# Gated attention and Mish layer on one core: Mish on 1024 columns, early heads kept in DRAM, VectorE exponentials in whole and half sets

## The chip, the core and the metric

The kernel runs on one core of a Trainium2 chip. The core has TensorE (PE, matrix products into PSUM banks of 512 32-bit columns), ScalarE (ACT, activation functions), VectorE (DVE, elementwise work), GpSimd (POOL) and SyncE (SP), which issues most DMAs. Each engine runs its own instructions strictly in the order in which the program lists them and waits on semaphores for the others. The metric is device time in microseconds (us) of one execution, the median of several runs; lower is better.

## The reference

```python
def _A_ref(x, wqkv, wo):            # H = 32 heads of Dh = 20, S = 2048, D = 640
    qkv = (x @ wqkv).reshape(B, S, 3, H, Dh).transpose(2, 0, 3, 1, 4)
    q, k, v = qkv[0], qkv[1], qkv[2]
    p = softmax(einsum("bhqd,bhkd->bhqk", q, k) * Dh ** -0.5, axis=-1)
    o = einsum("bhqk,bhkd->bhqd", p, v)
    return o.transpose(0, 2, 1, 3).reshape(B, S, D) @ wo

def _B_ref(x, w1, b1, w2):          # F = 1536
    h = einsum("bsd,df->bsf", x, w1) + b1
    sp = log1p(exp(-abs(h))) + where(h > 0, h, 0)
    return einsum("bsf,fd->bsd", h * tanh(sp), w2)

g = sigmoid((x * gate_w).sum(-1, keepdims=True))
return g * _A_ref(x, wqkv, wo) + (1 - g) * _B_ref(x, w1, b1, w2)
```

All inputs and the output are bf16. The activation `h * tanh(softplus(h))` is Mish. With n = e^h (e^h + 2) it is h * n / (n + 2), which is how the kernel computes it: one exponential and one reciprocal.

## The kernel before

**Attention.** The 32 heads are taken four at a time (p = 0 to 7) and the 2048 queries in four blocks qc of 512. A pair (p, qc) is a *group*; there are 32 groups G, first p = 0 to 5 with all four qc each, then for each qc the pairs p = 6 and p = 7. A group has 16 key blocks j of 128 keys and four heads t, 64 *units* in all. One unit is a score matmul (`Sp`, 128 keys by 512 queries, one PSUM bank), the exponential of it, and a matmul of V against the result, which adds into `acc` (L1160; V carries a column of ones, so the softmax sums come along). The maximum isn't subtracted; a bound on the scores is worked out on the way, and `attention_with_maximum` is a fallback that isn't entered with these inputs.

**The stream of iterations.** Units are packed into iterations that alternate between three and two banks of scores (`WIDTHS`, tiles `S0` and `S1`). Iteration i+1's scores are issued (`emit_qk`), then ScalarE takes iteration i's exponential in one instruction of 1536 or 1024 columns (`emit_exp`, L1108), then the V matmuls whose exponentials are issued (`emit_pv`), then VectorE work that is due, then fill-in matmuls on TensorE (`pump`).

**Heads on VectorE.** In groups 1 to 30 one key block of the 16 is left to VectorE: in some three-bank iterations ScalarE takes only two banks, and VectorE reads the third (`jv_read`, L735) into a 16-bit integer tile. When two heads are there, `jv_steps` makes the exponential from integer and 16-bit arithmetic, seven instructions on 128x1024 (L753 to L775). The score bank is free for the iteration after the next when both engines have read it.

**Other work between the iterations.** Projections of q, k, v, the Mish layer (`h_chain`, `mish_steps`, `b_chain`) and the output projection (`wo_chain`) are chains of matmul pieces with a start and a due iteration; `pump` places them in TensorE's order. VectorE's longer work is cut into steps with deadlines (`steps`, `run_slow`), which a planner with fixed costs (the list `T`) places into VectorE's order. Where TensorE would go quiet, matmuls of constants (`busy`, L1033) are put in. All of it is decided when the program is built, so every engine's order is fixed.

**Mish** works on one block of 128 rows of F by 512 tokens at a time: 12 blocks for each of four token blocks c. TensorE makes `h` (5 matmuls, L607), VectorE adds the bias (L618), ScalarE makes e^h (L548), and VectorE does nine instructions (L556 to L588): n and n + 2 in 32 bits, products of two and of four denominators so that only 128 columns need a reciprocal (L570), and the way back. The results lie in *cells* (48 tiles of 128x512 bf16). `b_chain` multiplies them with W2 and frees them.

**Outputs of heads.** At a group's end `normalise` turns `acc` over (L1128), divides by the sums and turns it back into a cell (L1146), which stays there until `wo_chain` uses it, late in the kernel, because the output projection of a query block needs all eight p.

Of the kernel before, what the change touches and what calls it, by code (L numbers as in the profile page):

```python
# [9 lines left out]
P = 128  # L10
# [31 lines left out]
def attention_with_maximum(tc, A_wqkv, b_dram, out2d, xT, VA, wo_sb, g_t, ident, pool):  # L42
# [10 lines left out]
    with tc.For_i(0, H, 1, name="heads") as h:  # L53
# [20 lines left out]
        with tc.For_i(0, S, P, name="queries") as q0:  # L74
# [9 lines left out]
            mx = pool["m"].tile([P, 4], F32, tag="r", name="mx")  # L84
# [23 lines left out]
            on = pool["m"].tile([P, DH], BF16, tag="h", name="on")  # L108
# [42 lines left out]
def kernel(  # L151
# [18 lines left out]
    FT = F // P  # L170
    NS = S // P
# [9 lines left out]
    JV_SETS = {G: 1 for G in range(1, 31)}  # L181
    JV_BIAS = 32
    JV_GAPS = {1: (4, 2, 4, 2), 2: (3, 2, 2, 2, 2, 2, 2, 2)}
    N_CAP = 1.0e9
    NCELL = 48
# [21 lines left out]
    mp = ctx.enter_context(tc.tile_pool(name="mp", bufs=2))  # L207
# [21 lines left out]
    E_dve = [consts.tile([P, 4, QC], BF16, tag=f"E_dve{i}", name=f"E_dve{i}") for i in range(2)]  # L229
    w_dve = consts.tile([P, 2, QC], F16, tag="w_dve")  # L230
    VB = consts.tile([P, 2, H, DH + 1], BF16, tag="VB")
    u_dve = consts.tile([P, 2, QC], F16, tag="u_dve")
    b_dram = tc.dram_tile([S, D], BF16, name="b_dram")
    acc = accpool.tile([P, QC], F32, tag="acc")
# [17 lines left out]
    def load_w1(k, eng=nc.sync):  # L252
        if k < 4 * NQC:
            i = k % 4
            w1t[k] = w1p.tile([P, KT, 3 * P], BF16, tag="w1t", name="w1t")
            eng.dma_start(out=w1t[k][:, :, :], in_=w1rows[:, :, 3 * P * i : 3 * P * (i + 1)])
# [43 lines left out]
    for G, (p, qc) in enumerate(groups):  # L300
        first.setdefault(p, G)

    mine_of = [[NS - 1 - k for k in range(JV_SETS.get(G, 0))] for G in range(len(groups))]
    units = [
        (G, p, qc, j, t)
        for G, (p, qc) in enumerate(groups)
        for j in range(NS)
        if j not in mine_of[G]
        for t in range(4)
    ]  # L310
    unit_at = {(G, j): k for k, (G, _, _, j, t) in enumerate(units) if t == 0}


# [3 lines left out]
    taken_by, iters_start = {}, {}  # L317
    while pos < len(units):
        i = len(iters)
        G = units[pos][0]  # L320
        n = min(WIDTHS[i % len(WIDTHS)], len(units) - pos)
        x = None
        got = taken_by.setdefault(G, [])
        sets_here = len(mine_of[G])
        if n == 3 and len(got) < 4 * sets_here:
            since = i - (got[-1][0] if got else iters_start.get(G, i))
            if since >= JV_GAPS[sets_here][len(got)] and units[pos + 1][0] == G:
                mine = {units[pos][4], units[pos + 1][4]}
                k, slot = divmod(len(got), 4)
                left = [t for t in range(4) if t not in [y for _, y in got[4 * k :]]]  # L330
                t = min(left, key=lambda t: (t in mine, t))
                got.append((i, t))
                x = (G, units[pos][1], k, t, slot)
                n = 2
        for k in range(pos, pos + n):
            iters_start.setdefault(units[k][0], i)
        iters.append((pos, n))
        extra.append(x)
        pos += n
    assert all(len(taken_by[G]) == 4 * len(mine_of[G]) for G in range(len(groups)))  # L340
# [17 lines left out]
    in_mish = [0]  # L358
    b_done = [0] * NQC
# [14 lines left out]
    NS_SCORES, NS_SET, NS_SCORES_SEEN, NS_EXP_SEEN, NS_MISH_EXP = 330.0, 320.0, 430.0, 180.0, 519.0  # L374
    NS_SEEN = 250.0
    QUEUE = 700.0
# [42 lines left out]
    def steps(start, parts, deadline, line=None):  # L419


        seq[0] += 1
        slow.append([deadline, seq[0], start, deque(parts), line])

# [120 lines left out]
    def mish_steps(ft, c, h):  # L545
        e = mp.tile([P, QC], F32, tag="e", name="e")
        r = mp.tile([P, QC], F32, tag="r", name="r")
        nc.scalar.activation(e[:, :], h[:, :], ACT.Exp)  # L548
        T["act"] += 519.0
        V = nc.vector  # L550
        d = r.rearrange("p (a b) -> p a b", a=2)
        Q = slice(0, P)

        def n_and_d():

            V.scalar_tensor_tensor(out=e, in0=e, scalar=2.0, in1=e, op0=ALU.add, op1=ALU.mult)  # L556
            V.tensor_scalar(out=r, in0=e, scalar1=N_CAP, scalar2=2.0, op0=ALU.min, op1=ALU.add)

        def products():

            V.scalar_tensor_tensor(
                out=e.rearrange("p (a b) -> p a b", a=2),
                in0=e.rearrange("p (a b) -> p a b", a=2),
                scalar=N_CAP, in1=d[:, ::-1, :], op0=ALU.min, op1=ALU.mult,
            )
            V.tensor_tensor(out=r[:, 2 * P :], in0=r[:, 0 : 2 * P], in1=r[:, 2 * P :], op=ALU.mult)
            V.tensor_tensor(out=r[:, Q], in0=r[:, 2 * P : 3 * P], in1=r[:, 3 * P :], op=ALU.mult)

        def invert():
            V.reciprocal(out=r[:, Q], in_=r[:, Q])  # L570

        def of_two():
            V.tensor_tensor(
                out=r[:, P : 3 * P].rearrange("p (a b) -> p a b", a=2),
                in0=r[:, 2 * P :].rearrange("p (a b) -> p a b", a=2)[:, ::-1, :],
                in1=r[:, Q].unsqueeze(1).to_broadcast([P, 2, P]),
                op=ALU.mult,
            )
            V.tensor_tensor(  # L579
                out=e.rearrange("p (a b) -> p a b", a=2),  # L580
                in0=e.rearrange("p (a b) -> p a b", a=2),
                in1=r[:, P : 3 * P].unsqueeze(1).to_broadcast([P, 2, 2 * P]),
                op=ALU.mult,
            )

        def last():
            t = taken.pop((ft, c))
            V.tensor_tensor(out=t, in0=h, in1=e, op=ALU.mult)  # L588
            act[(ft, c)] = t
            in_mish[0] -= 1  # L590
# [3 lines left out]
            [(1150, n_and_d), (1400, products), (920, invert), (1110, of_two), (690, last)],  # L594
            T["act"] + 9000.0,
        )

    def h_chain(ft, c, start, due):
        box = {}
        bank = opener(box, QC)  # L600

        def piece(kt):
            if kt == 0:
                in_mish[0] += 1
                taken[(ft, c)] = cells.pop()
# [3 lines left out]
                lhsT=w1t[4 * c + ft // 3][:, kt, (ft % 3) * P : (ft % 3 + 1) * P],  # L609
# [5 lines left out]
        def finish():  # L615
            h = mp.tile([P, QC], F32, tag="h", name="h")
            evac(740)
            nc.vector.tensor_scalar(  # L618
                out=h, in0=box["ps"][:, :], scalar1=b1f[:, ft : ft + 1], scalar2=None, op0=ALU.add
            )  # L620
            ready_h.append((T["dve"] + 200.0, lambda: mish_steps(ft, c, h)))
            if ft % 3 == 2:
                load_w1(4 * c + ft // 3 + 2)

        def ready():
            return in_mish[0] < 2 and len(cells) > CELLS_KEPT
# [43 lines left out]
    ots = {}  # L670
    wo_sb = [None]

    def wo_chain(s, half, start, due, ps_list, base=None, dst=None):
# [17 lines left out]
        def finish():  # L691
# [12 lines left out]
            if dst is None and half == 1:  # L704
                nc.sync.dma_start(out=out2d[s * P : (s + 1) * P, :], in_=ots[s][:, :])

        def ready():
            return all((p, c) in normalised for p in ps_list)
# [10 lines left out]
    jv_set = {}  # L719
# [3 lines left out]
    halves = {}  # L723
    jv_emitted = set()

    def jv_read(G, k, t, slot, ps, full):

        if slot == 0:
            n = jv_set[(G, k)] = len(jv_set)
            assert n < 2 or n - 2 in jv_emitted, (G, k)  # L730
        n = jv_set[(G, k)]
# [4 lines left out]
            out=E_dve[n % 2].bitcast(I16)[:, slot, :], in0=ps, scalar1=ROUND,  # L736
            scalar2=ROUND - 512.0 * JV_BIAS, op0=ALU.add, op1=ALU.subtract,
        )
        if slot % 2 == 1:
            left = (it_at(G + 1) - now[0]) * 1115.0  # L740
            due = T["act"] + (min(left - 4000.0, 9000.0) if k < len(mine_of[G]) - 1 else left - 4000.0)
            steps(T["dve"], jv_steps(G, k, slot // 2), due, "exp")

    def jv_steps(G, k, half):
        V = nc.vector
        E, w, u = (
            t.rearrange("p a n -> p (a n)")
            for t in (E_dve[jv_set[(G, k)] % 2][:, 2 * half : 2 * half + 2, :], w_dve, u_dve)
        )
# [24 lines left out]
        def scale():  # L774
            V.tensor_tensor(out=e, in0=e, in1=wi, op=ALU.add)  # L775
            halves[(G, k)] = halves.get((G, k), 0) + 1
            if halves[(G, k)] == 2:
                jv_at[(G, k)] = T["dve"] + NS_SEEN

        return [  # L780
            (380, mantissa), (380, exponent), (640, square), (380, factor), (380, factor2),
            (640, product), (640, scale),
# [155 lines left out]
    m0, m1 = it_at(1) + 10, it_at(G7[NQC - 1] - 1)  # L938
# [139 lines left out]
    def emit_qk(i):  # L1078
# [10 lines left out]
        if extra[i] is not None:  # L1089
            G, p, k, t, slot = extra[i]  # L1090
            todo.append((G, p, mine_of[G][k], t))
# [31 lines left out]
    def normalise(G, p, qc):  # L1123
# [20 lines left out]
        def turn():  # L1144
            normalised.add((p, qc))
            nc.vector.transpose(out=OT[(p, qc)][:, :], in_=t2[:, :])  # L1146

# [5 lines left out]
    jv_in = [0]  # L1153

    def emit_set(G, p, qc, j, moving, full, VB=None):
        n = pv_sets[0]
        T["pe"] = max(T["pe"], full, T["acc"] if n == 0 else 0.0) + NS_SET
        worked(T["pe"] - NS_SET, 215.0, 1.1)
        for t in range(4):
            nc.tensor.matmul(  # L1160
                acc[32 * t : 32 * t + DH + 1, :],
                lhsT=VA[:, j, 4 * p + t, :] if VB is None else VB[:, 4 * p + t, :],
                rhs=moving(t),
# [5 lines left out]
        if n == NS - 1:  # L1169
            normalise(G, p, qc)  # L1170
            pv_sets[0] = 0
            jv_in[0] = 0

    def emit_jv(G, p, qc):
        k = jv_in[0]
        n = jv_set[(G, k)]
        jv_in[0] += 1
        jv_emitted.add(n)
        E = E_dve[n % 2]
# [202 lines left out]
```

## Time and profile before

| | us |
|---|---|
| median of 3 runs | 934.8 (934.23 to 937.8) |
| the profiled execution | 934.48 |
| its span, first to last instruction | 932.7 |
| ScalarE busy | 908.5 |
| VectorE busy | 741.8 |
| TensorE busy (ends are modelled) | 866.7 |
| of that, matmuls of constants (L1033) | 110.3 |

A row of a group in the profile reads: line, engine, operation, output <- input by tile name, shapes and types, count; then the union of the busy time of the group in us and the mean ns of one instruction; then the idle time of the engine just before them with what ended it. A row of a window reads: stretch, its length, and for PE, PEld (weight load), DVE, ACT and POOL the busy us with the count of instructions, then the granted TensorE clock, the DMA share and GB/s. ScalarE's first exponential starts at 10.56 us and its last ends at 921.84 us; what follows is the last group's normalisation, projection and store. The granted TensorE clock is 0.996 of full speed.

### The profile page before, as it was taken

Reading aid. Unit: us, or ns where it says so; the run is one execution under the profiler, and the core shown is the slowest. Engines: PE = TensorE matmul, PEld = TensorE weight load, DVE = VectorE, ACT = ScalarE, POOL = GpSimd, SP = SyncE. Lnnn points to the kernel's source line nnn. Section 1 sums busy time; section 2 is a strip of 40 time slices with the busy share of each in tenths; the row PEclk is TensorE's granted clock in tenths of the full one; section 3 lists DMA queues with packets and bytes.
Section 4 is the critical chain, followed back from the end, with each engine's and each line's share of the span. In section 5 each row is a group of like instructions: output and inputs, shape, how many; then the busy total and the mean of one; then the engine's idle time right before and its main releaser. Section 6 shows DMA issues by size and latency. Waiting matters only on the chain.

```text
span 932.7 us, 15290 instructions
## 1 busy us (share of the span) xinstructions
PE 866.7 (93%) x6184; PEld 303.9 (33%) x6184; DVE 741.8 (80%) x1398; ACT 908.5 (97%) x873; POOL 24.4 (3%) x39
## 2 busy tenths in 40 slices
PE   8999999999999999999999999999999999999996
PEld 4433333223333333323332233233323233333332
DVE  4468888988888988889988889888888886786633
ACT  6999999999999999999999999999999999999995
POOL 5000100000000000000000000000000000000000
PEclk9999999999999999999999999999999999999998
DMA  9000100000100010001110001010000000100100
GB/s 270 32 1 1 31 1 22 17 6 1 31 1 22 2 31 1 22 1 50 29 23 16 22 1 31 3 48 2 21 1 22 1 9 8 43 8 9 43 29 31
DMA packets 25635, 22.00 MB, mean 24 GB/s; under 512 B 10088, under 2 KB 24312, under 8 KB 25560
## 3 DMA queue, kind: packets, MB, share of 16 engines
q1 hardware_dynamic: 22808, 14.28, 5.6%
q0 software_dynamic: 1520, 5.94, 2.1%
q8 instruction: 49, 0.80, 0.3%
q10 hardware_dynamic: 1232, 0.76, 0.3%
q14 instruction: 26, 0.21, 0.1%
HBM read 15.73 MB, written 5.24 MB: 22 GB/s over the span
## 4 chain that ended last, share of the span: by engine, by line
ACT 65%; issue 16%; PE 14%; DVE 3%; DMA 1%; POOL 1%; ACTq 0%; POOLq 0%
ACT E L1108 62%; PE Sp L1093 5%; ACT e L548 3%; PE acc L1160 3%; PE ps L638 2%; PE ps L490 2%; DMA wv<-in_A_wqkv_dram 1%; PE ps L683 1%; PE ps L607 1%; PE ps L1033 1%; PE ps L518 1%; DVE ot L1332 0%; DVE h L618 0%; POOL xs L273 0%; DVE T L1128 0%
## 5 line engine op out<-in xcount | busy, mean ns | idle before, releaser
L1108 ACT ACTIVATE E<-Sp 128x1024 bf16<-128x1024 f32 (+1 forms) x819 | 890.3, 1268 | 6.6 <-PE Sp L1093 3.7
L1093 PE MATMUL Sp<-qT,kT 32*128 32x512 bf16 x2048 | 326.1, 382 | 51.3 <-ACT E L1108 35.7
L1093 PEld LDWEIGHTS <-kT 32*128 32x128 bf16 x2048 | 108.6, 91 | 292.5 <-issue 253.8
L1160 PE MATMUL acc<-E,VA 128*21 128x512 bf16 x1928 | 191.2, 386 | 1.3 <-DVE T L1128 1.1
L735 DVE TENSOR_SCALAR E_dve<-Sp 128x512 int16<-128x512 f32 x120 | 82.8, 690 | 40.4 <-PE Sp L1093 39.5
L1033 PE MATMUL ps<-busy 128*128 128x512 bf16 x357 | 110.3, 384 | 0.0
L1160 PEld LDWEIGHTS <-VA 128*21 128x21 bf16 x1928 | 47.6, 88 | 108.8 <-issue 108.5
L607 PE MATMUL ps<-xT,w1t 128*128 128x512 bf16 x240 | 75.5, 385 | 0.0
L638 PE MATMUL ps<-w_sb,cell 128*128 128x320 bf16 x384 | 74.9, 302 | 0.0
L490 PE MATMUL ps<-xT,wkp 128*128 128x512 bf16 x155 | 48.4, 384 | 1.7 <-DVE xT L456 0.8
L490 PE MATMUL ps<-xT,wqp 128*128 128x512 bf16 x155 | 49.5, 384 | 0.0
L683 PE MATMUL ps<-wo_sb,cell 128*128 128x320 bf16 x248 | 48.2, 302 | 0.0
L618 DVE TENSOR_SCALAR h<-ps,b1f 128x512 f32<-128x512 f32 x48 | 35.8, 746 | 14.6 <-PE ps L607 14.1
L570 DVE RECIPROCAL r<-r 128x128 f32<-128x128 f32 x48 | 45.4, 946 | 0.6
L1128 DVE STREAM_TRANSPOSE T<-acc 128x512 f32<-128x512 f32 x32 | 22.9, 716 | 26.7 <-PE acc L1160 26.5
L772 DVE TENSOR_TENSOR w_dve<-w_dve,u_dve 128x1024 bf16<-128x1024 f16 x60 | 41.1, 685 | 0.9
L775 DVE TENSOR_TENSOR E_dve<-E_dve,w_dve 128x1024 int16<-128x1024 int16 x60 | 41.1, 685 | 0.9
L1033 PEld LDWEIGHTS <-busy 128*128 128x128 bf16 x357 | 26.9, 97 | 44.6 <-issue 35.1
L763 DVE TENSOR_TENSOR w_dve<-w_dve 128x1024 f16<-128x1024 f16 x60 | 41.0, 683 | 0.0
L638 PEld LDWEIGHTS <-cell 128*128 128x128 bf16 x384 | 29.3, 97 | 34.5 <-issue 28.0
L548 ACT ACTIVATE e<-h 128x512 f32<-128x512 f32 x48 | 34.9, 727 | 0.1
L579 DVE TENSOR_TENSOR e<-e,r 128x512 f32<-128x512 f32 x48 | 33.2, 692 | 1.6
(105 smaller groups left out, 651.1 us busy)
## 6 DMA issues: line engine op xcount, KB each, us to landing
w1t<-in_B_w_dram SPq DMA_DIRECT2D x14, 480.0 KB, 4.0
b_dram<-Bt SPq DMA_DIRECT2D x4, 640.0 KB, 3.2
out_dram<-ot SPq DMA_DIRECT2D x14, 160.0 KB, 1.8
xs<-in_A_x_dram POOLq DMA_DIRECT2D x3, 640.0 KB, 7.0
w_sb<-in_B_w_dram POOLq DMA_DIRECT2D x1, 1920.0 KB, 12.9
ws<-in_A_wqkv_dram SPq DMA_DIRECT2D x13, 100.0 KB, 4.0
w1t<-in_B_w_dram POOLq DMA_DIRECT2D x2, 480.0 KB, 8.8
wo_sb<-in_A_wo_dram SPq DMA_DIRECT2D x4, 200.0 KB
```

The costliest lines, as they stand in the source:

```text
L490: nc.tensor.matmul(box["ps"][:, :], lhsT=wpad[:, kt, :, :].rearrange("p h d -> p (h d)"), rhs=xT[:, kt, chunk * QC : (chunk + 1) * QC], st ...
L548: nc.scalar.activation(e[:, :], h[:, :], ACT.Exp)
L570: V.reciprocal(out=r[:, Q], in_=r[:, Q])
L607: nc.tensor.matmul(box["ps"][:, :], lhsT=w1t[4 * c + ft // 3][:, kt, (ft % 3) * P : (ft % 3 + 1) * P], rhs=xT[:, kt, c * QC : (c + 1) * QC ...
L638: nc.tensor.matmul(box["ps"][:, :], lhsT=act[(ft, c)][:, u * P : (u + 1) * P], rhs=w2_sb[:, ft, half * HALF : (half + 1) * HALF], start=(f ...
L683: nc.tensor.matmul(box["ps"][:, :], lhsT=OT[(p, c)][:, u * P : (u + 1) * P], rhs=wo_sb[0][:, p, cols], start=(k == 0), stop=(k == len(ps_l ...
L735: S_reader[0] = nc.vector.tensor_scalar(out=E_dve[n % 2].bitcast(I16)[:, slot, :], in0=ps, scalar1=ROUND, scalar2=ROUND - 512.0 * JV_BIAS, ...
L772: V.tensor_tensor(out=w.bitcast(BF16), in0=w, in1=u, op=ALU.mult)
L1033: nc.tensor.matmul(ps[:, 0:n], lhsT=busy[:, :], rhs=busy_row(n), start=True, stop=True)
L1093: nc.tensor.matmul(ps[:, k * QC : (k + 1) * QC], lhsT=kT[p][32 * t : 32 * t + 32, j * P : (j + 1) * P], rhs=qT[G][32 * t : 32 * t + 32, :] ...
L1108: exp = nc.scalar.activation(E[:, 0 : n * QC], S_of.pop(i)[:, 0 : n * QC], ACT.Exp, scale=LN2 / 512.0)
L1160: nc.tensor.matmul(acc[32 * t : 32 * t + DH + 1, :], lhsT=VA[:, j, 4 * p + t, :] if VB is None else VB[:, 4 * p + t, :], rhs=moving(t), st ...
```

## The change

- *Heads on VectorE.* Groups 1 to 31 have one whole set of four heads (key block 15). The groups 1, 2, 4, 5 and every second one to 29, sixteen in all, have a half set too: two heads of key block 14, whose other two heads stay on ScalarE. A set is computed when all its heads are read, on 128x2048 (whole) or 128x1024 (half), in the same seven steps. The units' head order now turns with the key block, and the head that VectorE takes is always another than the two beside it. A whole set's V matmuls go in when it is ready, a half set's at the group's end.
- *Mish* works on two blocks of 128 rows at once, 1024 columns: `h` is bf16, one exponential for both, n + 2 in fp16, the way back in 16 bits where marked. The reciprocal still takes 128 columns at a time. The buffers other than `h` exist once instead of twice, so the next pair's exponential is issued only after `share` of the one before (`mish_free`). W1 is loaded in tiles of 256 columns instead of 384.
- *Outputs of heads* p = 0 to 5 are stored to DRAM (`heads_dram`, 128 KB each, 24 in all) by SP right after they are normalised, and loaded back eight iterations before the group of p = 7 of their query block. There are 40 cells instead of 48.
- *The planner* has new costs, a longer look-ahead for VectorE's steps (`QUEUE`) and later deadlines.

```diff
-    JV_SETS = {G: 1 for G in range(1, 31)}
+    JV_DOUBLE = (1, 2, *range(4, 5), *range(5, 30, 2))
+    JV_PARTS = {G: 2 if G in JV_DOUBLE else 1 for G in range(1, 32)}
+    JV_HEADS = (4, 2)
-    JV_GAPS = {1: (4, 2, 4, 2), 2: (3, 2, 2, 2, 2, 2, 2, 2)}
-    N_CAP = 1.0e9
-    NCELL = 48
+    JV_GAPS = {1: (6, 2, 2, 2), 2: (5, 2, 2, 2, 2, 2)}
+    N_CAP = 16382.0
+    NCELL = 40
...
-    mp = ctx.enter_context(tc.tile_pool(name="mp", bufs=2))
+    mp = ctx.enter_context(tc.tile_pool(name="mp", bufs=1))
+    hp = ctx.enter_context(tc.tile_pool(name="hp", bufs=2))
...
+            ts = [(j + k) % 4 for k in range(4)]
+            if j == NS - 2 and JV_PARTS.get(G, 0) > 1:
+                ts = [t for t in ts if t not in heads_of[(G, 1)]]
...
-    QUEUE = 700.0
+    QUEUE = 1400.0
+    MISH_DUE, JV_DUE, NS_ITER = 22000.0, 22000.0, 1080.0
...
+        e = mp.tile([P, 2 * QC], F32, tag="e", name="e")
+        d = mp.tile([P, 4, 2 * P], F16, tag="d", name="d")
+        d2 = mp.tile([P, 2, 2 * P], F32, tag="d2", name="d2")
+        d4 = mp.tile([P, 2 * P], F32, tag="d4", name="d4")
+        r2 = mp.tile([P, 2, 2 * P], BF16, tag="r2", name="r2")
+        nc.scalar.activation(e[:, :], h[:, :, :].rearrange("p a n -> p (a n)"), ACT.Exp)
...
+        r = d2.rearrange("p a n -> p (a n)").bitcast(F16)
+        y = d.rearrange("p a n -> p (a n)").bitcast(BF16)
+        def n():
             V.scalar_tensor_tensor(out=e, in0=e, scalar=2.0, in1=e, op0=ALU.add, op1=ALU.mult)
         def products():
+            V.tensor_scalar(
+                out=d.rearrange("p a n -> p (a n)"), in0=e, scalar1=N_CAP, scalar2=2.0,
+                op0=ALU.min, op1=ALU.add,
+            )
+            V.tensor_tensor(out=d2, in0=d[:, 0:2, :], in1=d[:, 2:4, :], op=ALU.mult)
+        def invert(half):
+            cols = slice(half * P, (half + 1) * P)
+            if half == 0:
+                V.tensor_tensor(out=d4, in0=d2[:, 0, :], in1=d2[:, 1, :], op=ALU.mult)
+            V.reciprocal(out=d4[:, cols], in_=d4[:, cols])
         def of_two():
             V.tensor_tensor(
+                out=r2, in0=d2[:, ::-1, :], in1=d4.unsqueeze(1).to_broadcast([P, 2, 2 * P]),
                 op=ALU.mult,
             )
+        def of_one():
             V.tensor_tensor(
+                out=r.rearrange("p (b a n) -> p b a n", b=2, a=2),
+                in0=d.rearrange("p (b a) n -> p b a n", b=2)[:, ::-1, :, :],
+                in1=r2.unsqueeze(1).to_broadcast([P, 2, 2, 2 * P]),
                 op=ALU.mult,
             )
+        def share():
+            V.scalar_tensor_tensor(out=y, in0=e, scalar=N_CAP, in1=r, op0=ALU.min, op1=ALU.mult)
+            mish_free[0] = True
+        def last(half):
...
+            V.tensor_tensor(out=t, in0=h[:, half, :], in1=y[:, half * QC : (half + 1) * QC], op=ALU.mult)
...
-        if slot % 2 == 1:
...
+        if slot == JV_HEADS[k] - 1:
+            left = (it_at(G + 1) - now[0]) * NS_ITER
+            steps(T["dve"], jv_steps(G, k), T["act"] + left - JV_DUE, "exp")
...
         def turn():
-            normalised.add((p, qc))
             nc.vector.transpose(out=OT[(p, qc)][:, :], in_=t2[:, :])
+            if p < NQ - 2:
+                cell = OT.pop((p, qc))
+                nc.sync.dma_start(out=o_dram[p, qc], in_=cell[:, :])
+                at(now[0] + 4, lambda: cells.insert(0, cell))
+            else:
+                normalised.add((p, qc))
...
+    def fetch(p, qc):
+        if not cells:
+            at(now[0] + 2, lambda: fetch(p, qc))
+            return
+        OT[(p, qc)] = cells.pop()
+        nc.sync.dma_start(out=OT[(p, qc)][:, :], in_=o_dram[p, qc])
+        at(now[0] + 6, lambda: normalised.add((p, qc)))
+    for qc in range(NQC):
+        for p in range(NQ - 2):
+            at(it_at(G7[qc]) - 8 + 2 * p, lambda p=p, qc=qc: fetch(p, qc))
...
-        while ready_h and ready_h[0][0] <= T["act"]:
+        while ready_h and mish_free[0] and ready_h[0][0] <= T["act"]:
```

In the changed program the reads of scores are L799, the seven exponential steps L814 to L836, and Mish's steps L603 (`n`), L606 and L610 (`products`), L615 and L616 (`invert`), L619 (`of_two`), L625 (`of_one`), L633 (`share`) and L639 (`last`).

## The prediction

> **What bounds the kernel now.** I read the busy shares, then the chain that ended last, then ScalarE's groups by shape, then windows by stage, then who waits for whom.
>
> ```profile
> PE 866.7 (93%) x6184; PEld 303.9 (33%) x6184; DVE 741.8 (80%) x1398; ACT 908.5 (97%) x873; POOL 24.4 (3%) x39
> ...
> ACT 65%; issue 16%; PE 14%; DVE 3%; DMA 1%; POOL 1%; ACTq 0%; POOLq 0%
> ```
>
> ScalarE is busy 97% of the 932.7 us span and holds 65% of the chain. Its work is three groups (first time column: union in us, second: mean ns of one):
>
> ```profile
> L1108 ACT ACTIVATE E<-Sp 128x1024 bf16<-128x1024 f32 x529 | 548.5, 1120 | 5.7 <-PE Sp L1093 2.8 <-PE acc L1160 2.0
> L1108 ACT ACTIVATE E<-Sp 128x1536 bf16<-128x1536 f32 x290 | 445.8, 1537 | 0.9 <-PE Sp L1093 0.8
> L548 ACT ACTIVATE e<-h 128x512 f32<-128x512 f32 x48 | 34.9, 727 | 0.1
> ```
>
> Neighbours overlap, so a record is longer than the time it takes from the queue. The timeline of ScalarE shows it (start, length):
>
> ```profile
> 405.05 0.62 ACT L548 ACTIVATE e<-h 128x512 f32<-128x512 f32 x1
> 405.57 6.87 ACT L1108 ACTIVATE E<-Sp 128x1024 bf16<-128x1024 f32 x6
> ```
>
> From one start to the next, a Mish exponential takes 0.52 us, while its mean record is 727 ns: 0.21 us overlaps. The difference of the two E rows, 1537 - 1120 = 417 ns, has the overlap cancelled: it is the price of one more 512-column head. By stage (PE, PEld, DVE, ACT busy us):
>
> ```profile
> 200.00:400.00 200.00, 186.72 (x1280) 63.15 (x1280) 175.02 (x323) 199.85 (x195) 0.98 (x2) 1.00 0.05 13
> ...
> 826.00:912.00 86.00, 85.04 (x641) 32.35 (x640) 50.17 (x94) 84.72 (x77) 0.00 (x0) 1.00 0.06 22
> ```
>
> In the middle ScalarE never rests and VectorE is busy 87.5%; in the last three groups TensorE is as full as ScalarE. The waits (total us, times, longest):
>
> ```profile
> DVE E_dve L735 <- PE Sp L1093: 39.5, 85, 1.1
> ...
> PE Sp L1093 <- ACT E L1108: 35.7, 136, 0.7
> ...
> ACT E L1108 <- PE Sp L1093: 3.7, 9, 0.8
> ```
>
> VectorE reached 85 of its 120 reads of scores early, by 0.46 us on average: it has room now.
>
> **1. ScalarE: heads moved away.** 120 heads on VectorE become 31 x 4 + 16 x 2 = 156. In the listings the number of E exponentials stays 819, but 254 are 1536 wide and 565 are 1024 wide: 36 fewer heads at 0.417 us = **-15.0 us**, on the bounding engine.
>
> **2. ScalarE: Mish in pairs.** 48 x 0.52 = 25.0 us becomes 24 of 128x1024. No row shows one from SBUF with 16-bit input. Bounds: the PSUM row less the overlap above, 1120 - 207 = 0.91 us; twice the 512 case, 1.04 us. I take 0.52 + 0.417 = 0.94, since the extra columns cost that in the E rows: 22.5 us, **-2.5 us** (-3.1 to 0). The Trainium skill (ScalarE: Activation LUTs, What ACT_TABLE_LOAD costs) gives 186 ns plus 0.833 ns a column less 93 ns of overlap, the same rate in both types: an estimate of 0.946 us, and the saving would be 2.3. At 512 its figure, 0.520, is the trace's.
>
> **3. VectorE.** Rows of before:
>
> ```profile
> L570 DVE RECIPROCAL r<-r 128x128 f32<-128x128 f32 x48 | 45.4, 946 | 0.6
> L772 DVE TENSOR_TENSOR w_dve<-w_dve,u_dve 128x1024 bf16<-128x1024 f16 x60 | 41.1, 685 | 0.9
> ...
> L579 DVE TENSOR_TENSOR e<-e,r 128x512 f32<-128x512 f32 x48 | 33.2, 692 | 1.6
> ...
> L556 DVE SCALAR_TENSOR_TENSOR e<-e 128x512 f32<-128x512 f32 x48 | 32.6, 680 | 0.0
> L758 DVE TENSOR_SCALAR E_dve<-E_dve 128x1024 int16<-128x1024 int16 x60 | 25.5, 425 | 1.4
> ...
> L557 DVE TENSOR_SCALAR r<-e 128x512 f32<-128x512 f32 x48 | 20.5, 426 | 1.7
> L566 DVE TENSOR_TENSOR r<-r 128x256 f32<-128x256 f32 x48 | 20.4, 425 | 1.7
> ```
>
> 512 columns against 256 (692, 425) give 1.04 ns a column for 32-bit tensors; the 16-bit two-tensor row (685 at 1024) fits half of that and the 16-bit scalar row (425) a quarter, over some 155 ns each. Mish before, nine rows (680, 426, 684, 425, 292, 946, 418, 692, 686): 5.25 us, x48 = 252.0. After, for a pair: L603 680 + 533 = 1213; L606 426 + 267 = 693; L610 692 (its output is 32-bit; at least 418); L615 425; L616 2 x 946; L619 692; L625 685; L633 1213; L639 2 x 418: 8.34 us, x24 = 200.2, **-51.8**. Two rows are unproved, L625 and L639, two-tensor operations with mixed 16-bit types: between 685 and 1213, and 418 and 686; I take the low ends because L772, all 16-bit, lies there. A third is L606, 32-bit in and 16-bit out: 693, or 1213 at the worst. By the Trainium skill (Vector Engine (DVE) Microarchitecture Reference, 5.1 Performance modes) two elements a cycle need only that all tensors have 2 bytes and step by one; L772 agrees, mixed types no row shows, and its list of things not measured has an operand read backwards, as L625 reads its blocks. By it the low ends hold.
>
> Exponentials: 36 reads more at 690 (L735) = +24.8. Before, a set of four was two halves of 4 x 423 + 3 x 684 = 3.74 us. After, 31 sets at 2048 columns, 4 x 690 + 3 x 1218 = 6.41 (the slopes above), and 16 halves at 3.74: 258.7 against 60 x 3.74 = 224.6, +34.1. Net +7.1 us of rows. VectorE's records also overlap, some 35 ns each (rows add to about 790, their union is 741.8); 237 fewer instructions take 8 us of that away. Busy: about 757 us.
>
> That costs nothing as long as ScalarE covers it: in a stretch of 28.5 us (one group) VectorE now has 24.9 (175.02/200); with 15/30 more it needs 25.4, while ScalarE's group shrinks to about 27.9: 91%. The order listing supports the split: Mish rows of 4 to 7 us fall in groups with a half set, 8 to 12 in those without, and no group's rows add to more than 28.3 (before: 29.9). What is no longer free is lateness. TensorE may overwrite a score bank only after ScalarE's exponential and VectorE's read (L799), so a late read delays scores, and ScalarE behind them. There are 36 more reads, and instructions of 1.2 us can stand ahead of them where 0.69 was the most. Bounds: 0 to 156 x (1.218 - 0.685) = 83 us if nothing covered; 0.46 us of earliness and a 0.9 us exponential cover most. I take **+1.5**.
>
> **4. New wait on ScalarE.** The Mish buffers exist once, so the exponential of pair m+1 waits until L633 of pair m has read `e`. Behind it stand all E exponentials, and TensorE behind them. In VectorE's order the next L603 comes 3 to 43 instructions after L633, within 6 in 5 of 23 pairs. Bounds 0 to 5 x 1.0 = 5; I take **+1**.
>
> **5. TensorE at the end.** Groups 29 to 31 hold 85.04 of 86 us. They lose 6 heads on ScalarE (2.5 us), but on TensorE, by the listings, only 5 matmuls of 320 columns, one set of four and 3 fillers, about 1.1 us. The rest of the gain is lost there: **+1.4** (0 to 2.5). The 60 fillers that go (L1033, 357 to 297) were off the path.
>
> **6. Queues.** SP gets 24 stores of 128 KB and 24 loads; the W1 transfers become 24 of 320 KB from 16 of 480. A store waits for VectorE's transpose, with W1, strips and the next store behind it; W1 is wanted one pair later, some 30 us. Rows show 1.8 us (160 KB out) to 4.0 us to landing; a load has 6 iterations of about 1.1 us before its head counts as there. Cost 0; without that cover a batch of six is 6 x 2 = 12 us on the output projections. Mish of the last block ends in group 28 as before, although there are 40 cells for 48.
>
> **Sum.** The profiled execution took 934.5 us (1.8 around its span), the median is 934.8. 934.5 - 15.0 - 2.5 + 1.5 + 1.0 + 1.4 = 920.9; I say **920**, the 417 being a little short of a start-to-start price.
>
> **Rivals.**
> - *Fewer stalls* (0.12). The E records run from 10.56 to 921.84 us in the timeline, 911.3 us; less 0.21 us of overlap each, wide rows take 1.33, narrow ones 0.91, and with Mish at 0.52 they add to 290 x 1.33 + 529 x 0.913 + 48 x 0.52 = 894: some 17 us are small stalls. If half vanish and nothing of points 3 to 5 comes: 934.5 - 17.5 - 8.5 = 908.5. For it: 237 fewer instructions of VectorE, and as many hand-overs. Against: the full TensorE at the end and 36 more reads.
> - *Late reads* (0.18): 0.08 us on each of 156 reads, 12 us: 930. For it: 35 of 120 reads are already not early. Against: ScalarE waits for scores only 3.7 us now.
> - *Slower: the 16-bit rows run at the 32-bit rate* (0.12), so that the change does not do what it says. Place: L606, L625, L639: 520 + 528 + 2 x 268 = 1.58 us a pair, 38 us. A group then needs 25.4 + 1.5 and, in order, waits of 0.33 us at each of 5 reads: 28.5, above ScalarE's 27.9, and with the 0.8 us at L1188 29.4: VectorE sets the pace, 0 to 0.9 us a group over 27 groups, 935 to 957; 943. It decides from 1.5 us more per group. Against: L772.
> - *Spilled heads come late* (0.05): 12 us at the end, 932.
> - *Forecast* (0.53): 914 to 926.
>
> **Chances.** What one can tell from no change here is about 0.5% (930.1 to 939.5). Faster 0.80 (forecast, fewer stalls, most of late reads); same 0.08; slower 0.12. Range 909 to 934; the ends leave about 0.04 and 0.14.
>
> **What would show it.** ScalarE's E rows x254 and x565 with means as before; Mish records x24 near 1.14 us; L625 near 685 and L639 near 420; L799's wait for scores well over 0; ScalarE busy 97% or more. TensorE's scores waiting for VectorE rows, or VectorE above 93% between 200 and 750 us, would make me wrong.

## The result, and the profile after

The changed kernel takes 920.7 us in the median (918.46 to 922.18, 4 runs), the kernel before 935.4 on the same chip; the ratio is 0.984, 95% interval 0.981 to 0.987. The profiled executions took 918.46 and 934.48 us, 16.0 us apart.

The busy shares and the chain of the changed kernel, from its page:

```profile
PE 847.1 (92%) x6124; PEld 298.9 (33%) x6124; DVE 751.2 (82%) x1175; ACT 892.7 (97%) x849; POOL 26.4 (3%) x39
...
ACT 70%; issue 14%; PE 11%; DVE 3%; DMA 1%; POOL 1%; ACTq 0%; POOLq 0%
```

ScalarE still sets the pace, at the same 97%, and VectorE does 9.4 us more work in 16 us less time. ScalarE's groups by shape (union in us, mean ns of one, idle before):

```profile
L1168 ACT ACTIVATE E<-Sp 128x1024 bf16<-128x1024 f32 x565 | 575.1, 1112 | 4.5 <-PE Sp L1153 2.3 <-ACT E L1168 0.2 <-PE acc L1228 0.2
L1168 ACT ACTIVATE E<-Sp 128x1536 bf16<-128x1536 f32 x254 | 392.3, 1544 | 0.9 <-PE Sp L1153 0.8
L596 ACT ACTIVATE e<-h 128x1024 f32<-128x1024 bf16 x24 | 27.6, 1151 | 0.2
```

36 exponentials have become one head narrower, and Mish's are 24 at 1.15 us. The timeline of ScalarE has what one of those takes from the queue (start, length):

```profile
426.29 1.30 ACT L596 ACTIVATE e<-h 128x1024 f32<-128x1024 bf16 x1
427.24 31.70 ACT L1168 ACTIVATE E<-Sp 128x1024 bf16<-128x1024 f32 x30
```

0.95 us from start to start. The trace's start-to-start times give the whole account. Undisturbed, an exponential takes 1.330 us (three heads), 0.904 (two), 0.519 (Mish before) or 0.946 (Mish in pairs); anything above that I call a stall of ScalarE.

| us | before | after | difference |
|---|---|---|---|
| first E exponential starts | 10.56 | 11.23 | +0.7 |
| undisturbed times of all exponentials but the last | 887.5 | 870.0 | -17.5 |
| stalls of ScalarE | 22.2 | 22.9 | +0.7 |
| of these in groups 29 to 31 | 4.8 | 5.5 | +0.7 |
| from the end of the last exponential to the end | 10.9 | 11.1 | +0.2 |
| span | 932.7 | 916.6 | -16.1 |

The last exponential's own record, some 1.5 us in both, makes up the rest of the span. Everything that was gained is ScalarE's own work, and almost nothing was given back. VectorE's rows that the prediction had to estimate:

```profile
L836 DVE TENSOR_TENSOR E_dve<-E_dve,w_dve 128x2048 int16<-128x2048 int16 x31 | 38.2, 1232 | 0.8
...
L633 DVE SCALAR_TENSOR_TENSOR d<-e,d 128x1024 bf16<-128x1024 f32 x24 | 29.2, 1218 | 0.4
...
L639 DVE TENSOR_TENSOR cell<-h,d 128x512 bf16<-128x512 bf16 x48 | 18.8, 418 | 0.5
...
L610 DVE TENSOR_TENSOR d<-d 128x512 f32<-128x512 f16 x24 | 16.8, 698 | 0.8
...
L625 DVE TENSOR_TENSOR d<-d,r 128x1024 f16<-128x1024 f16 x24 | 16.7, 694 | 0.4
L606 DVE TENSOR_SCALAR d<-e 128x1024 f16<-128x1024 f32 x24 | 16.4, 681 | 0.3
```

L625 (694 ns) and L639 (418) lie at the low ends that were taken, beside the all-16-bit row of before (685 at 1024 columns). Windows by stage (PE, PEld, DVE, ACT busy us), the first in the middle, the second on the last three groups:

```profile
200.00:400.00 200.00, 184.26 (x1286) 61.86 (x1282) 176.39 (x261) 199.92 (x193) 0.99 (x2) 1.00 0.07 17
...
810.00:896.00 86.00, 85.34 (x642) 31.85 (x639) 55.15 (x87) 85.06 (x79) 0.00 (x0) 1.00 0.13 42
```

VectorE is 88.2% busy in the middle, where it was 87.5%, and TensorE is again full at the end. VectorE's wait for scores, in the list of waits:

```profile
DVE E_dve L799 <- PE Sp L1153: 56.6, 80, 2.6
```

80 of its 156 reads were early, by 0.7 us on average. From this line I would still say that it has room. The experiments show that added work costs time from the first instruction on.

### The profile page after: what moved, and what is told of

The parts are those of the page before. It is cut to its first block, busy times and chain, and to the rows that moved or that the text cites. A ratio compares the mean times of both kernels' runs of the same rounds, so it can differ in the third digit from the quotient of the medians.

```text
span 916.6 us, 15023 instructions
## 1 busy us (share of the span) xinstructions
PE 847.1 (92%) x6124; PEld 298.9 (33%) x6124; DVE 751.2 (82%) x1175; ACT 892.7 (97%) x849; POOL 26.4 (3%) x39
## 3 DMA queue, kind: packets, MB, share of 16 engines
q10 hardware_dynamic: 1232, 0.76, 0.3%
## 4 chain that ended last, share of the span: by engine, by line
ACT 70%; issue 14%; PE 11%; DVE 3%; DMA 1%; POOL 1%; ACTq 0%; POOLq 0%
ACT E L1168 67%; PE Sp L1153 4%; ACT e L596 2%; PE acc L1228 2%; PE ps L529 1%; PE ps L699 1%; PE ps L745 1%; DMA wv<-in_A_wqkv_dram 1%; PE ps L666 1%; DVE ot L1433 0%; PE ps L557 0%; DVE d L633 0%; DVE w_dve L824 0%; POOL xs L283 0%; DVE T L1188 0%
## 5 line engine op out<-in xcount | busy, mean ns | idle before, releaser
L1168 ACT ACTIVATE E<-Sp 128x1024 bf16<-128x1024 f32 (+1 forms) x819 | 871.2, 1246 | 5.4 <-PE Sp L1153 3.1
L1153 PE MATMUL Sp<-qT,kT 32*128 32x512 bf16 x2048 | 321.3, 382 | 53.3 <-ACT E L1168 38.3
L799 DVE TENSOR_SCALAR E_dve<-Sp 128x512 int16<-128x512 f32 x156 | 107.3, 688 | 57.4 <-PE Sp L1153 56.6
L1093 PE MATMUL ps<-busy 128*128 128x512 bf16 (+1 forms) x297 | 94.7, 384 | 0.0
L836 DVE TENSOR_TENSOR E_dve<-E_dve,w_dve 128x2048 int16<-128x2048 int16 (+1 forms) x47 | 49.3, 1048 | 1.3
L833 DVE TENSOR_TENSOR w_dve<-w_dve,u_dve 128x2048 bf16<-128x2048 f16 (+1 forms) x47 | 48.9, 1040 | 1.1
L824 DVE TENSOR_TENSOR w_dve<-w_dve 128x2048 f16<-128x2048 f16 (+1 forms) x47 | 48.6, 1034 | 0.0
L616 DVE RECIPROCAL d<-d 128x128 f32<-128x128 f32 x48 | 44.5, 939 | 0.8
L676 DVE TENSOR_SCALAR h<-ps,b1f 128x512 bf16<-128x512 f32 x48 | 35.5, 740 | 9.4 <-PE ps L666 9.2
L1188 DVE STREAM_TRANSPOSE T<-acc 128x512 f32<-128x512 f32 x32 | 22.9, 715 | 17.2 <-PE acc L1228 17.1
L1093 PEld LDWEIGHTS <-busy 128*128 128x128 bf16 x297 | 22.2, 97 | 39.8 <-issue 34.4
L557 PE MATMUL ps<-wv,xT 128*128 128x80 bf16 (+2 forms) x240 | 33.1, 258 | 0.3 <-DVE xT L495 0.3
L544 DVE CAST kT<-ps 128x512 bf16<-128x512 f32 x31 | 21.2, 682 | 13.3 <-PE ps L529 13.1
```

The source lines that it names most:

```text
L799: S_reader[0] = nc.vector.tensor_scalar(out=E_dve[k].bitcast(I16)[:, slot, :], in0=ps, scalar1=ROUND, scalar2=ROUND - 512.0 * JV_BIAS, op0 ...
L824: V.tensor_tensor(out=w, in0=w, in1=w, op=ALU.mult)
L833: V.tensor_tensor(out=w.bitcast(BF16), in0=w, in1=u, op=ALU.mult)
L1093: nc.tensor.matmul(ps[:, 0:n], lhsT=busy[:, :], rhs=busy_row(n), start=True, stop=True)
L1153: nc.tensor.matmul(ps[:, k * QC : (k + 1) * QC], lhsT=kT[p][32 * t : 32 * t + 32, j * P : (j + 1) * P], rhs=qT[G][32 * t : 32 * t + 32, :] ...
L1168: exp = nc.scalar.activation(E[:, 0 : n * QC], S_of.pop(i)[:, 0 : n * QC], ACT.Exp, scale=LN2 / 512.0)
```

## The experiments

Each ratio is against the kernel before on the same chip; its medians there are 935.1 to 936.5 us. "VectorE" is its busy time in the profile, "Mish done" the start of the last instruction that writes a Mish result (L588 before, L639 after), "tail" the time from the end of ScalarE's last exponential (of Mish in the runs with five more and with half sets everywhere) to the end of the span, "constants" the matmuls of constants that `pump` put in, counted by their weight loads. Line numbers are each kernel's own.

| kernel | VectorE, us | constants | Mish done, us | stalls, us | tail, us | median, us | ratio to before (95%) |
|---|---|---|---|---|---|---|---|
| before | 741.8 | 357 | 833 | 22.2 | 10.9 | 935.4 | 1 |
| after | 751.2 | 297 | 818 | 22.9 | 11.1 | 920.7 | 0.984 (0.981 to 0.987) |
| heads as before | 670.4 | 311 | 816 | 21.5 | 11.2 | 935.8 | 1.000 (0.997 to 1.002) |
| Mish as before | 801.2 | 541 | 913 | 27.0 | 33.4 | 946.9 | 1.010 (1.007 to 1.013) |
| one VectorE instruction more per group | 765.6 | 425 | 860 | 31.3 | 16.4 | 930.9 | 0.993 (0.991 to 0.996) |
| two more | 783.2 | 495 | 893 | 32.0 | 23.3 | 939.6 | 1.003 (1.000 to 1.005) |
| five more | 833.6 | 540 | 951 | 61.2 | 41.1 | 986.1 | 1.053 (1.049 to 1.058) |
| half set in every group | 825.5 | 536 | 963 | 85.8 | 41.1 | 1004.6 | 1.073 (1.069 to 1.077) |

The third column belongs to every reading below: an edit to VectorE's work also changes how many matmuls of constants the planner puts into TensorE's list.

### Which part of the change makes the gain?

**Heads as before, Mish in pairs kept:**

```diff
-    JV_DOUBLE = (1, 2, *range(4, 5), *range(5, 30, 2))
-    JV_PARTS = {G: 2 if G in JV_DOUBLE else 1 for G in range(1, 32)}
+    JV_DOUBLE = ()
+    JV_PARTS = {G: 2 if G in JV_DOUBLE else 1 for G in range(1, 31)}
```

> The changed kernel with the heads on VectorE as before (one whole set in groups 1 to 30, 120 heads), all else kept. Theory A (the time is the sum of ScalarE's start-to-start times plus about 45 us of start, end and small stalls): 36 heads at 0.417 us come back, 15 us more than the changed kernel's 920.7, or 2 to 3 us less than the kernel before because Mish in pairs stays: 933 to 936. Theory B (a good part of the gain comes from VectorE's 237 fewer instructions, so fewer stalls of ScalarE): 925 to 930, with ScalarE's stalls clearly under 22 us.

935.8 us, no difference from the kernel before that these runs can tell; the stalls are 21.5 us. Theory A holds, theory B falls. The median hides some 3 us: the profiled execution, at a mean clock of 0.993, has a span of 929.3 us, 3.4 less than before, of which 2.2 are Mish's exponentials, and the ten executions ran at 0.980 to 0.993. The busy line of this run:

```profile
PE 855.6 (92%) x6138; PEld 303.1 (33%) x6138; DVE 670.4 (72%) x1020; ACT 905.7 (97%) x849; POOL 24.5 (3%) x39
```

VectorE works 71 us less than before, in 378 fewer instructions, and the time is the same: room on VectorE is worth nothing by itself while ScalarE has the same heads to do.

**Mish as before, the 156 heads kept:** `mish_steps` and `h_chain` are those of the kernel before, with W1 in the new tiles and the new deadlines.

```diff
-    mp = ctx.enter_context(tc.tile_pool(name="mp", bufs=1))
-    hp = ctx.enter_context(tc.tile_pool(name="hp", bufs=2))
+    mp = ctx.enter_context(tc.tile_pool(name="mp", bufs=2))
...
-    def mish_steps(m, c):
+    def mish_steps(ft, c, h):
```

> The changed kernel with Mish as before (one block of 512 columns at a time, 32-bit, two buffers), 156 heads on VectorE kept. Theory A alone (ScalarE's sum): only the 2.2 to 2.5 us of the Mish exponentials come back: 923. Theory C (Mish in pairs pays through VectorE: its 52 us of rows are what makes room for the 36 heads): VectorE needs about 1.9 us more per group, 27 us of ScalarE's 27.5, and with its waits it becomes the pace-maker in the middle: 930 to 945, ScalarE's stalls in groups 2 to 27 rise from 14 us to 20 or more.

946.9 us: slower than the kernel before, although ScalarE has 15.3 us less to do. Theory A alone is out by 24 us. Theory C has the direction, and its 20 us of stalls in groups 2 to 27 are there (20.9 us, for 13.5 in the changed kernel), but they are the smaller part: all stalls went from 22.9 to 27.0 us only. The other 22 us come after the stream. The timeline of its end (start, length; the longest pieces):

```profile
913.32 0.69 DVE L626 TENSOR_TENSOR cell<-h,e 128x512 bf16<-128x512 f32 x1
914.07 11.72 PE L677 MATMUL ps<-w_sb,cell 128*128 128x320 bf16 x85 [1.70 <-DVE cell L626]
...
925.63 7.77 PE L723 MATMUL ps<-wo_sb,cell 128*128 128x320 bf16 x56
```

The last Mish result is written when ScalarE's stream is over (911.2 us). Only then can TensorE multiply the last token block with W2, and only then comes the output projection of it: 20 us of matmuls which the changed kernel does under the exponentials. The tail is 33.4 us for 11.1.

Neither part alone gains anything in the median; together they gain 15 us. The heads take the time off ScalarE, and Mish in pairs takes the work off VectorE that makes it possible. What the 244 matmuls of constants that this run has more than the changed kernel cost was not taken apart; the tail, by the timeline, waits for VectorE's last Mish result.

### How much room is left on VectorE?

Instructions without a use, a 16-bit multiply of 128x1024, were added to the changed kernel in groups 2 to 27 (here two):

```diff
+        if 2 <= G <= 27:
+            steps(T["dve"], [(690, more)] * 2, T["dve"] + MISH_DUE, "more")
+
+    def more():
+        nc.vector.tensor_tensor(out=fill[:, 1, :], in0=fill[:, 0, :], in1=fill[:, 0, :], op=ALU.mult)
```

**One per group (18 us):**

> The changed kernel with one more VectorE instruction in each of the groups 2 to 27 (0.69 us each, 18 us in all), between the changed kernel and the run with two more (36 us, 19 us slower). If the changed kernel stands right at the edge of VectorE's room, the loss is in proportion: 6 to 12 us, 927 to 933, with the last Mish cell 30 us or more later than at 818 us of the changed kernel. If there are 18 us of room left: 920 to 923.

**Two (36 us):**

> The changed kernel with two more VectorE instructions in each of the groups 2 to 27 (16-bit multiply of 128x1024 constants, 0.69 us each, result unused, placed by the planner), 1.4 us a group, 36 us in all. Theory A with room left on VectorE: 0 to 2 us slower than 920.7. If VectorE is already at its limit (point of decision at or under 1.4 us a group): its 36 us show almost in full, 940 to 955.

**Five (89 us):**

> As the run with two more, but five a group: 3.4 us a group, 89 us in all. Past the point of decision that the prediction put at 1.5 us a group: VectorE needs about 28.3 us a group (25 now) against ScalarE's 27.5, plus its waits for reads: 0.8 to 2 us a group over 26 groups, 940 to 970. If VectorE's waits are all given up when it is late, only 0.8 x 26 = 21 us: 942. If it still has room: under 925.

Against the changed kernel's median they cost 10, 19 and 65 us. One more came out as expected of a kernel at the edge of VectorE's room (927 to 933), two more a little under the 940 to 955 named, five more above its range of 940 to 970. One, two and five more move the last Mish result to 860, 893 and 951 us, and the tail from 11.1 to 16.4, 23.3 and 41.1 us. Stalls in groups 2 to 27 rise as well, from 13.5 to 22.5 us with one more and 25.1 with two. With five the Mish exponential itself waits at the end: 19.4 us in 4 waits.

ScalarE's list is the same in all three, but TensorE's is not. The groups of matmuls of constants, changed kernel and one more:

```profile
L1093 PE MATMUL ps<-busy 128*128 128x512 bf16 (+1 forms) x297 | 94.7, 384 | 0.0
L1094 PE MATMUL ps<-busy 128*128 128x512 bf16 x425 | 132.5, 386 | 0.0
```

So the 12.3 us between the two profiled spans (929.0 and 916.6) are not all VectorE's room. The tail has 5.3 of them: 42 matmuls of the output projection are left when the stream ends. 4.8 are stalls in a stretch of 6.8 us at half clock (779.4 to 786.2), which follows TensorE's wait of 1.8 us for a cast of VectorE (L925; in the changed kernel this wait is 1.1 us, with no such stretch behind it). 3.5 are other stalls, in which ScalarE waits for TensorE's scores and V matmuls; and the stream starts 1.3 us earlier. TensorE's scores wait for VectorE's reads only 0.3 us. The 3.5 us are about what added matmuls of constants cost alone: 143 more, in the last run below, go with 4 us. The tail goes with the later end of Mish in all three runs, and returns to 11.5 us when Mish is put first, as the run with that order below shows. How the stalls divide between VectorE's lateness and TensorE's longer list stays open.

**A half set in every group**, 30 heads more:

```diff
-    JV_DOUBLE = (1, 2, *range(4, 5), *range(5, 30, 2))
+    JV_DOUBLE = tuple(range(1, 32))
```

> The changed kernel with a half set in every group 1 to 31 (186 heads on VectorE). Theory A alone: 30 heads more off ScalarE, 12.8 us less: 908. Theory C: 15 more half sets at 3.74 us and 30 reads at 0.69, 77 us more VectorE work, which the groups that also hold most of Mish can't take: 925 to 945, VectorE over 93% busy between 200 and 750 us, scores waiting for VectorE's reads.

1004.6 us, 60 us beyond theory C's range, at a mean granted clock of 0.956 to 0.969. Its list of waits names the wait that the single Mish buffers brought:

```profile
ACT e L596 <- DVE d L633: 51.1, 5, 18.1
```

Five Mish exponentials, the last ones, wait 51 us on ScalarE for VectorE's `share` (L633); all of it falls in the last group, where the stalls are 53.3 of 85.8 us. In the middle VectorE was at most 88% busy, where theory C expected over 93%, and the stalls of groups 2 to 27 are some 27 us for 13.5: the backlog of Mish has grown until it meets the end of the stream.

### Where does VectorE's overflow go?

**Mish first:** two instructions more per group, and the deadlines of Mish and of the added instructions put ahead of those of the exponentials.

```diff
-    MISH_DUE, JV_DUE, NS_ITER = 22000.0, 22000.0, 1080.0
+    MISH_DUE, JV_DUE, NS_ITER = -30000.0, 22000.0, 1080.0
```

> The run with two more VectorE instructions per group, with one edit: the deadlines of Mish's steps and of the added instructions lie ahead of those of the exponentials, so Mish is never put off. Theory E (what VectorE cannot do in time is put off by the planner onto Mish, whose last block then keeps the projections, and the end, waiting): the last Mish cell comes back from 893 us to under 840, the stretch after ScalarE's last exponential from 23 us to 11 or 13, and ScalarE's stalls before it grow instead, from 32 us to 45 or more, as exponentials of VectorE come late; the time stays at 930 to 950. Rival (the end is late because TensorE is full there, whatever Mish does): the stretch stays over 20 us.

The tail is back at 11.5 us, so the rival, a full TensorE at the end, falls, and the stalls rose from 32 to 164 us, as theory E says. But the time is 1057.9 us (ratio 1.126, 1.120 to 1.133), far over its range, and Mish is done at 942 us because everything before it is stretched. The waits:

```profile
ACT E L1169 <- PE Sp L1154: 74.1, 71, 6.2
PE acc L1234 <- DVE E_dve L837: 60.3, 26, 4.2
ACT E L1169 <- PE acc L1234: 57.7, 28, 7.9
```

TensorE's V matmuls wait for VectorE's exponentials 26 times, and ScalarE then waits for scores and for its output buffers. But a second cause comes with it. Two neighbouring windows at the first such waits (the clock is the last figure but two):

```profile
100.60:104.00 3.40, 0.40 (x4) 0.10 (x4) 3.23 (x7) 0.91 (x1) 0.00 (x0) 1.00 0.00 0
104.00:107.40 3.40, 1.68 (x10) 0.31 (x9) 3.24 (x5) 0.00 (x0) 0.00 (x0) 0.50 0.00 0
```

TensorE stands almost still, and then its clock is halved. Before ScalarE's stream ends, 253 us pass at half clock, and 144 of the 164 us of stalls lie in such stretches; the mean granted clock is 0.877. So a microsecond of overflow cost 0.5 us with Mish put off to the end (18.9 us for 36), and 3.8 when the exponentials were late (137.2 us for the same 36), but the 3.8 are lateness and slow clock together, and no run takes them apart.

### Other parts

**The spill to DRAM alone**, put into the kernel before:

```diff
-    NCELL = 48
+    NCELL = 40
...
+            if p < NQ - 2:
+                cell = OT.pop((p, qc))
+                nc.sync.dma_start(out=o_dram[p, qc], in_=cell[:, :])
+                at(now[0] + 4, lambda: cells.insert(0, cell))
```

> The kernel before with the outputs of heads p = 0 to 5 stored to DRAM and loaded back and with 40 cells, nothing else changed. Theory A: no cost and no gain, within 1.5 us of the kernel before (935.4). Rival (late reloads or a blocked SP queue): output projections wait, ScalarE or TensorE stalls in groups 26 to 31, 5 to 12 us more.

934.7 us, ratio 0.998 (0.994 to 1.001): no cost. Its stores and loads of heads have the same lines as the changed kernel's; the last column is us from issue to landing, well within the six iterations allowed:

```profile
heads_dram<-cell SPq DMA_DIRECT2D x24, 128.0 KB, 1.7
cell<-heads_dram SPq DMA_DIRECT2D x24, 128.0 KB, 2.5
```

**More half sets at the end**, where VectorE is about 60% busy (groups 28, 30 and 31 added):

> The changed kernel with half sets also in groups 28, 30 and 31 (6 heads more on VectorE), where VectorE is only some 60% busy. Theory A alone: 6 x 0.426 = 2.6 us less than the changed kernel. Theory D (TensorE sets the pace in groups 28 to 31): ScalarE's stalls there grow by as much as its work falls, gain 0 to 1 us.

919.8 us, ratio 0.982 (0.979 to 0.985), against 0.984: within 1 us of the changed kernel. The undisturbed exponentials fell by 2.6 us and the stalls rose by 4.2, of which 2.8 in group 27 and 1.4 in group 12, where this execution has stretches at half clock; groups 29 to 31 hold 5.8 us of stalls, little over 5.5. The time is what theory D expected, but not for its reason: the 2.6 us go into the tail, 13.7 us for 11.1. The timeline around the stream's end at 906.4 us:

```profile
905.13 3.45 PE L745 MATMUL ps<-wo_sb,cell 128*128 128x320 bf16 x23
...
907.04 0.68 DVE L836 TENSOR_TENSOR E_dve<-E_dve,w_dve 128x1024 int16<-128x1024 int16 x1
...
908.74 0.38 PE L1228 MATMUL acc<-E_dve,VB 128*21 128x512 bf16 x2
```

VectorE finishes group 31's half set 1.3 us after the stream, and its V matmuls stand behind 23 matmuls of the output projection.

**Half sets moved from group 27 to 28, 30 and 31:**

```diff
-    JV_DOUBLE = (1, 2, *range(4, 5), *range(5, 30, 2))
+    JV_DOUBLE = (1, 2, 4, *range(5, 26, 2), 28, 29, 30, 31)
```

> Half sets taken from group 27 and given to groups 28, 30 and 31: 160 heads on VectorE instead of 156. Theory A with room at the end: 4 heads at 0.426 us, 1.7 us less, and Mish's last cell a little earlier; 917 to 920. Theory D (TensorE sets the pace there): 919 to 922, the same as the changed kernel within its scatter.

917.7 us, ratio 0.979 (0.975 to 0.983). Mish is done at 806 us, 12 us earlier, and the stalls in groups 29 to 31 are 4.1 us. This is the fastest kernel of the study; the intervals overlap with the changed kernel's, so that it is better is likely, and not shown. Its tail is 12.4 us, with a half set in group 31 here too.

**Mish begun earlier as well** (`MLP_FROM, MLP_TO = 2, 2`, half sets of 25 and 27 left out):

> As the run with half sets moved to the end, but without those of groups 25 and 27 (158 heads) and with the Mish layer begun eight iterations earlier and its schedule ended one group earlier. If the end is held up by Mish's last block: last Mish cell before 810 us, ScalarE's stalls in groups 29 to 31 fall from 5.5 us by 2 to 4, 914 to 918. If TensorE's amount of work there decides: 919 to 923.

925.4 us, ratio 0.987 (0.983 to 0.991), a miss. The end did what was expected: Mish is done at 788 us and the stalls of groups 29 to 31 fall from 5.5 to 2.5 us. But group 3 now stalls for 5.7 us instead of 1.2, in a stretch of 10 us at half clock from 104 us on.

**More matmuls of constants** (143 more), on the kernel with half sets moved:

```diff
-    FLOOR = 0.54
+    FLOOR = 0.57
```

> The run with half sets moved from group 27 to the end, and one constant changed: the floor of TensorE's activity below which the planner puts in matmuls of constants is 0.57 instead of 0.54 (some 90 such matmuls more). In the runs so far a kernel's times spread over 4 to 10 us in step with the mean granted clock, and the profiles of the longer ones show one or two stretches of 3.4 or 6.8 us at half clock, near 350 and 780 us. Theory F (such a stretch follows when TensorE has been idle too long, and costs about 2 us each): all runs at a mean clock of 0.995 or more, spread under 1.5 us, 916 to 918. Rival (the stretches come whatever TensorE does): the same spread, 916 to 923. If the added matmuls stand in the way of scores: ScalarE's stalls over 27 us and 919 or more at full clock.

920.4 us (920.27 to 921.25), ratio 0.984 (0.982 to 0.986). The spread is gone, with a mean clock of 0.994 to 0.996 in all runs, so theory F holds for the spread; but at full clock it is 4 us slower than the same kernel with fewer (916.3 to 916.4 at 0.995 or more, on another chip, where the fastest execution of the kernel before took 933.8 us, for 933.3 here), as the last case expected, though with 25.7 us of stalls, under the 27 named. Mish is done at 831 us for 806. The added matmuls cost more than the slow stretches they prevent.

## Why the prediction was right

*Heads moved away, -15.0:* right. The start-to-start times of the two E shapes did not change, 1.330 and 0.904 us, so 36 heads are -15.3.

*Mish exponentials, -2.5:* right; 0.95 us each, as the 0.94 taken, and -2.2 in all. The estimate that the prediction worked out from the Trainium skill (ScalarE: Activation LUTs, What ACT_TABLE_LOAD costs), 0.946 us, is the trace's time to the ns.

*VectorE's rows:* right. The rows named here were within 2%: L603 1213 (1213 taken), L633 1218 (1213), L625 694 (685), L610 698 (692), the 2048-column steps 689 to 692 and 1215 to 1232 (690 and 1218). Busy 751 for 757. VectorE's instructions fell by 223 (1398 to 1175), not 237; at the 35 ns each that were taken this is 0.5 us of busy time.

*Late reads, +1.5, and the new wait, +1:* mis-sized; both cost next to nothing. Stalls in groups 0 to 28 are 17.4 us in both kernels, and ScalarE sits idle 0.2 us in front of the 24 Mish exponentials. The wait is real when VectorE is late, as 51 us in the run with half sets everywhere show.

*TensorE at the end, +1.4:* half the size, +0.7 us (4.8 to 5.5 in groups 29 to 31).

*Queues, 0:* right; the spill is shown by the run with it alone, W1's smaller tiles by the run with the heads as before, which has them and is no slower.

The sum was 920.9 against a profiled 918.5; the three terms are 3.2 us too much, and a later first exponential and a longer tail, which it didn't have, take 0.9 of that back. That 920 meets the median, 920.7, so closely is partly luck: the three terms stand against a slower clock in two of the four executions, 0.989 and 0.990, which took 922.2 and 921.6 us.

What failed lies beside the sum. The prediction said that VectorE's extra work costs nothing at 91% of ScalarE's time, and put the point from which it decides at 1.5 us more per group. The first is true of this kernel only because the change adds no more than 9 us net; the second is not borne out: 0.7 us per group costs 10 us, part of it perhaps through TensorE's longer list. The slower rival expected VectorE to set the pace of the middle; the runs show that the middle loses 7 to 12 us (groups 2 to 27 in the old Mish, one and two more), while the work that VectorE cannot do slides, Mish first, until the last token block's matmuls fall behind ScalarE's stream and add 5 to 22 us there. Nor is it the reads of scores that come late: with one and two more per group, TensorE's scores wait for them 0.3 and 0.6 us in all. And the sign that I read as room, early reads in VectorE's wait list, is no measure of it: in an order fixed beforehand an engine waits at some places and is behind at others. With two instructions more per group, VectorE still waited 49.8 us at the same reads. A better sign may be the time at which the lowest-priority chain is done, 833 us before, against the time at which its consumers need it; it goes with the tail in the table's rows, but no forecast was made by it.

## What to carry to other kernels

Work moved off the bounding engine pays in full only if the engine that takes it has room, and making that room pays nothing by itself: here the two halves of one change were worth 0 and -10 us apart, and 15 together. Measure room by adding dummy work of the same kind and watching the end of the chain with the lowest priority; a busy share of 88%, or waits that look like slack, did not show what the added work would cost. Look at what else such an edit changed: here a planner answered each instruction on VectorE with more matmuls on TensorE. When work must be put off, let it be the work with the most time before its reader; here that was the cheaper order.

## What the runs showed of the hardware

The granted TensorE clock falls to half for stretches of 3.4 us or a multiple in some executions, and two executions of one kernel differ by it. In the profile of the kernel with half sets moved to the end, windows before and in such a stretch (the clock is the last figure but two):

```profile
346.60:350.00 3.40, 2.67 (x22) 0.77 (x15) 3.33 (x7) 3.40 (x4) 0.00 (x0) 1.00 0.17 45
350.30:353.70 3.40, 3.13 (x13) 0.74 (x12) 3.13 (x4) 2.48 (x3) 0.00 (x0) 0.53 0.53 119
```

ScalarE, busy throughout before, works 2.48 of 3.4 us. In the 3.4 us that end where the stretch begins (347.1 to 350.5 us) TensorE was busy for 2.17 us, and in the changed kernel, which has no such stretch there, for 2.94. The same figure is 1.61 us ahead of the stretch at 779.4 us with one VectorE instruction more, 1.39 ahead of the one at 103.9 us with Mish begun earlier, and 0.40 in the first one with Mish first: TensorE need not stand still for the whole 3.4 us. In the run with the heads as before, ten executions go from 931.2 us at a mean clock of 0.993 to 941.1 at 0.980, some 0.8 us for each 0.001; the runs at 0.995 or more of the kernel with moved half sets agree within 0.1 us. The Trainium skill (TensorE: Matmul & The Clock Gate, Part 1) has the two rates and the length of the window, 3.4 us, and ties the slow one to an idle TensorE; the trace agrees with the length, and the figures just given, like the run with 143 more matmuls, which has no such stretch before the end of ScalarE's stream, agree with the cause. How busy TensorE must be to keep its clock no run here shows.
